# Second half of the scores in a folding bank, and the operand tile 384 bytes further on

## The chip, the cores and the metric

The kernel runs on one core of a Trainium2 chip. The metric is the device time of one execution in microseconds, as the median of several runs. Engines are named as the profile names them: PE is the matrix engine (PEld its weight loads, which overlap its matmuls), DVE the vector engine, ACT the scalar engine, POOL and SP the two others; SP issues all the DMAs here. PSUM is the memory that PE writes, in eight banks of 512 fp32 columns; SBUF is the memory that it reads.

## The reference

Three layers follow one another. Attention goes through 32 memory slots for each of 4 x 8 heads; then come a feed-forward layer with a squared ReLU, and four small feed-forward layers weighted by the probabilities of a domain:

```python
a = softmax(phi, axis=2)                       # (4, 8, 576, 32)
k_m, v_m = a^T k, a^T v                        # (4, 8, 32, 64)
attn = softmax(q k_m^T / 8)                    # (4, 8, 576, 32)
x = heads_joined(attn v_m)                     # (2304, 512)
h = relu(x @ w_in);  x = (h * h) @ w_out       # 512 -> 2048 -> 512
for e in range(4):                             # 512 -> 1024 -> 512 each
    out += p[:, e] * (relu(x @ w1[e]) @ w2[e])
```

## The kernel before

Every large product is made of three matmuls on float32r operands: a value is split into a high part and a rest, and high x high, high x rest and rest x high are summed in PSUM. So each tile of operands holds a high and a low half.

**Stage one** (0 to about 120 us) takes the attention in 8 groups of 4 heads (2 groups for each of the 4 batches). `attention(g)` has a front, up to its `yield`, and a back. The front makes the softmax over phi, transposes it on PE (L132), multiplies it with k and v (L139), transposes that (L156), and makes the scores in two halves of 288 columns (L169, two matmuls each). Each half lands in a bank with the tag `score`, of which there is one, and DVE turns it into the tile `st` (L173). The back is the softmax over the scores on DVE and ACT, up to `at`, which is split into the attention's high part (ACT, L191) and low part (DVE, L192). `fold(s, b)` multiplies v_m into slab s of w_in for batch b: PE matmuls into two banks with the tag `fold` (L296), and a split on ACT and DVE (L302, L303). `first_l1` (L320) multiplies the folded weights with the attention, and `first_l2` (L342) multiplies its squared ReLU with w_out. The string PROGRAM gives the order in which fronts (F), backs (B), folds (A), first-layer pieces (U) and chunks of weights (W) are written; the build's scheduler then puts the instructions of each engine in their final order by the dependences and the free banks. Weights of the first layer come as 64-bit floats that DVE turns into fp32 (L206 to L218), seven instructions a chunk.

**Stage two** (about 120 to 403 us) runs the other slabs of the first layer. **Stage three** (403 us to the end) runs the four domain layers in 16 slabs, each done twice, for 1024 tokens at a time (and 256 left over in the second turn). There `second_pair` makes seven products of 6 matmuls of 512 columns each (L470): the moving operand is one of the slots b11, b21, t1 ... b22, which lie in the tile `mem`, the stationary one is a weight tile `w` or `ws`. `second_rest` (L516) does the same for the tokens left over, 256 columns wide, also from `mem`. `second_l2` (L431) follows, with the weights as moving operand, 512 columns, and DVE adds the outcome to `acc` (L442).

`mem` is the operand tile of all that: 73,728 bytes in each partition of SBUF, first the attention and the folded weights of the 4 batches, later the nine slots of stage three. In the built program of before it begins at byte 17,024 of each partition, which is 33 x 512 + 128; `acc` comes right behind it. All slots are multiples of 8,192 bytes from its beginning, and each of their moving operands is 2,048 bytes long, so each of these starts 128 bytes behind a multiple of 512. The tiles of weights and those of `g`, `gh`, `gl` begin at multiples of 512 (in stage two and three).

Of the kernel before, what the change touches and what calls it, by code (L numbers as in the profile page):

```python
# [12 lines left out]
F32 = mybir.dt.float32  # L13
# [8 lines left out]
NT, DM, DFF, E, F2 = 2304, 512, 2048, 4, 1024  # L22
# [16 lines left out]
def tile_kernel(  # L39
# [11 lines left out]
    const = ctx.enter_context(tc.tile_pool(name="const", bufs=1))  # L51
# [8 lines left out]
    def bank(tag):  # L60
        return ps.tile([128, 512], F32, tag=tag, name=tag, bufs=BANKS[tag])

    ident = const.tile([128, 128], F32, name="ident")
    make_identity(nc, ident)

# [5 lines left out]
    slot = [mem[:, i * 4 * NB:(i + 1) * 4 * NB] for i in range(9)]  # L73
    acc = const.tile([128, NT * KT], F32, name="acc")
    yacc = acc.rearrange("p (k n) -> p k n", k=KT)
    p_sb = const.tile([128, NT // 128, E], F32, name="p_sb")
    p_sum = const.tile([128, NT // 128], F32, name="p_sum")


    FIRST_LOADS = "p0 q0 r0 k0 p1 r1 k1 q1 r2 r3"  # L80
# [1 line left out]


    PROGRAM = (
        "F0 W W F1 B0 A0 B1 F2 U0 W W F3 U1 B2 A1 B3 F4 U2 F5 U3 W B4 A2 B5 F6 U4 W F7 U5 "
        "B6 A3 B7 W U6 W U7"
    )


# [27 lines left out]
    def attention(att, g):  # L117
        b, hg = divmod(g, 2)
        ph, kvt, qt = phs[g], kvs[g], qs[g]
        nmax = att.tile([128, 1], F32, tag="nmax", name="nmax")  # L120
        nc.vector.tensor_reduce(out=nmax, in_=ph, axis=AX.X, op=ALU.max, negate=True)
        esum = att.tile([128, 1], F32, tag="esum", name="esum")
        nc.scalar.activation(ph, ph, AF.Exp, bias=nmax, scale=1.0, accum_out=esum)
        rs = att.tile([128, 1], F32, tag="rs", name="rs")
        nc.vector.tensor_scalar_add(rs, esum, 1e-9)
        nc.vector.reciprocal(rs, rs)
        en = att.tile([128, len(CH), 128], F32, tag="en", name="en", bufs=1)
        pa = bank("turn")
        pb = bank("memory")
        for c, (s0, n) in enumerate(CH):  # L130
            dst = pa[:n, c * 128:(c + 1) * 128] if c < 4 else pb[:n, :128]
            nc.tensor.transpose(dst, ph[:, s0:s0 + n], ident)  # L132
        nc.scalar.copy(en[:, 0:4].rearrange("p c m -> p (c m)"), pa)
        nlast = CH[-1][1]
        nc.scalar.copy(en[:nlast, 4], pb[:nlast, :128])
        kvp = pb[:, 128:256]
        for c, (s0, n) in enumerate(CH):
            for h in range(4):
                nc.tensor.matmul(  # L139
                    kvp[h * M:(h + 1) * M, :2 * D],  # L140
                    en[:n, c, h * M:(h + 1) * M],
                    kvt[c][:n, :, h, :],
                    start=(c == 0),
                    stop=(c == len(CH) - 1),
                )


        kvd = att.tile([128, 2, 2, D], F32, tag="kvd", name="kvd", bufs=1)
        nc.scalar.activation(
            kvd,  # L150
            kvp.rearrange("p (v d) -> p v d", v=2).unsqueeze(2).to_broadcast([128, 2, 2, D]),
            AF.Copy, scale=rs,
        )
        kt = pb[:, 256:512]
        for v in range(2):
            nc.tensor.transpose(kt[:, v * 128:(v + 1) * 128], kvd[:, v].rearrange("p z d -> p (z d)"), ident)  # L156
        bt = bdk[g % 2]
        ktv = kt.rearrange("p (v z e m) -> p v z e m", v=2, z=2, e=2)
        for e in range(2):
            rows = slice(e * D, (e + 1) * D)  # L160
            nc.scalar.copy(bt[rows, :, e * M:(e + 1) * M], ktv[rows, 0, :, e, :])
        rows = slice(hg * D, (hg + 1) * D)
        nc.scalar.copy(vt[rows, b], kt[rows, 128:])
        st = att.tile([128, S // 32, 32], F32, tag="st", name="st", bufs=2)
        stf = st.rearrange("p j m -> p (j m)")
        for z in range(2):
            sc = bank("score")
            for pr in range(2):
                nc.tensor.matmul(  # L169
                    sc[pr * 64:(pr + 1) * 64, :HS], bt[:, pr, :], qt[pr][:, z * HS:(z + 1) * HS],  # L170
                    start=True, stop=True,
                )
            nc.vector.transpose(out=stf[:, z * HS:(z + 1) * HS], in_=sc[:, :HS])  # L173
        yield
        mx = att.tile([128, S // 32], F32, tag="mx", name="mx")
        nc.vector.reduce_max(out=mx, in_=st, axis=AX.X)
        nc.vector.tensor_tensor(
            out=st, in0=st, in1=mx.unsqueeze(2).to_broadcast([128, S // 32, 32]), op=ALU.subtract
        )
        nc.scalar.activation(st, st, AF.Exp, scale=1.0 / math.sqrt(D))  # L180
        sm = att.tile([128, S // 32], F32, tag="sm", name="sm")
        nc.vector.reduce_sum(out=sm, in_=st, axis=AX.X)
        nc.vector.tensor_scalar_add(sm, sm, 1e-9)
        nc.vector.reciprocal(sm, sm)
        nc.vector.tensor_tensor(
            out=st, in0=st, in1=sm.unsqueeze(2).to_broadcast([128, S // 32, 32]), op=ALU.mult
        )
        at = att.tile([128, S], F32, tag="at", name="at", bufs=1)
        nc.vector.transpose(out=at, in_=stf)
        hi = atts[b][:, hg]  # L190
        nc.scalar.copy(hi, at)  # L191
        nc.vector.tensor_tensor(out=atts[b][:, 2 + hg], in0=at, in1=hi.bitcast(F32), op=ALU.subtract)  # L192
# [347 lines left out]
    with tc.tile_pool(name="bdp", bufs=1) as bdp, tc.tile_pool(name="cv", bufs=1) as cv, \  # L540
# [6 lines left out]
        with tc.tile_pool(name="att", bufs=2) as att, tc.tile_pool(name="hp1", bufs=2) as hp, \  # L547
# [3 lines left out]
            def front(g):  # L551
                if g not in phs:
                    phs[g] = load_phi(att, g)
                if g not in kvs:
                    kvs[g] = load_kv(att, g)
                if g not in qs:
                    qs[g] = load_q(g)
                at[g] = attention(att, g)
                next(at[g])
# [129 lines left out]
```

## Time and profile before

| | us |
|---|---|
| median of 3 runs | 1167.53 |
| lowest, highest | 1166.3, 1167.62 |
| time of the profiled execution | 1166.94 |
| its span, first to last instruction | 1164.9 |
| PE busy in it | 1139.3 |
| DVE busy in it | 839.0 |
| ACT busy in it | 494.9 |

The span is the part of the time that the trace shows; 2.0 us of the profiled execution's time lie around it. Busy time is added up over the whole span, so an engine that is busy for 72% of it can still be the one that sets the pace in a stage. An end of a matmul is modelled in the trace, so the pace of matmuls is read from start to start.

### The profile page before, as it was taken

What the parts mean: (1) busy time and instruction counts of PE and PEld (TensorE: products, weight loads), DVE (VectorE), ACT (ScalarE), POOL (GpSimd) and SP (SyncE); (2) the same over time, 40 slices, a digit from 0 to 9 for tenths busy, and PEclk for the clock granted to TensorE, in tenths of its full rate; (3) what the DMA queues carried; (4) which work ended last, traced back from release to release, by engine and by line L of the source; (5) the groups of instructions that cost most, each with busy time, mean ns of one, the idle gap of its engine ahead of it and who ended that gap; (6) DMA issues with size and microseconds to landing.
All of it is one profiled execution on the core that took longest, in us unless ns stands there. A gap on an engine that the chain in (4) does not pass through costs nothing.

```text
span 1164.9 us, 16690 instructions
## 1 busy us (share of the span) xinstructions
PE 1139.3 (98%) x6520; PEld 957.9 (82%) x6520; DVE 839.0 (72%) x1442; ACT 494.9 (42%) x1051; POOL 121.3 (10%) x136
## 2 busy tenths in 40 slices
PE   5899999999999999999999999999999999999998
PEld 2676898999999988888888888888888888888886
DVE  5988999887457667777777778856666666666654
ACT  2666555544466563343433434543333333332321
POOL 0000000001010022121121211211111111121000
PEclk9799999999999999999999999999999999999999
DMA  9751222211000111111111111311111111111002
GB/s 313 237 184 37 73 74 91 74 55 55 1 19 1 54 46 64 37 55 55 55 55 37 55 55 53 110 37 37 37 37 54 37 55 37 37 37 37 19 1 91
DMA packets 25599, 72.68 MB, mean 62 GB/s; under 512 B 2992, under 2 KB 3504, under 8 KB 25520
## 3 DMA queue, kind: packets, MB, share of 16 engines
q1 hardware_dynamic: 25520, 71.61, 18.5%
q8 instruction: 51, 0.84, 0.3%
q14 instruction: 28, 0.23, 0.1%
HBM read 66.88 MB, written 4.72 MB: 61 GB/s over the span
## 4 chain that ended last, share of the span: by engine, by line
PE 91%; DVE 6%; ACT 1%; issue 1%; DMA 1%; SPq 0%; ACTq 0%
PE moe L470 23%; PE fold L431 17%; PE memory L431 8%; PE moe L342 8%; PE turn L431 8%; PE moe L320 4%; PE moe L516 4%; PE score L470 4%; PE turn L342 2%; PE score L342 2%; PE memory L342 2%; PE fold L296 2%; PE memory L320 1%; PE score L320 1%; PE memory L139 1%; DVE acc L350 1%
## 5 line engine op out<-in xcount | busy, mean ns | idle before, releaser
L431 PE MATMUL fold<-w,g 128*128 128x512 f32 x864 | 221.4, 391 | 0.0
L470 PE MATMUL moe<-mem,ws 128*128 128x512 f32 x768 | 201.4, 397 | 0.8 <-DVE c L478 0.8
L431 PEld LDWEIGHTS fold<-w,g 128*128 128x128 f32 x864 | 160.2, 188 | 33.2
L470 PEld LDWEIGHTS moe<-mem,ws 128*128 128x128 f32 x768 | 142.7, 188 | 37.9 <-DVE c L478 5.4
L342 PE MATMUL moe<-gh,wo 128*128 128x288 f32 x576 | 130.8, 298 | 1.2 <-ACT acc L348 0.7
L442 DVE SCALAR_TENSOR_TENSOR acc<-fold,p_sb,acc 128x512 f32<-128x512 f32 x135 | 100.8, 747 | 40.4 <-PE fold L431 40.2
L266 POOL TENSOR_TENSOR s<-ra 128x256 f32<-128x256 f32 x32 | 27.2, 850 | 951.5 <-DVE ws L232 391.3
L483 ACT COPY cc<-moe 128x512 f32<-128x512 f32 x96 | 56.1, 584 | 149.6 <-PE moe L470 149.4
L431 PE MATMUL turn<-w,g 128*128 128x512 f32 x432 | 110.1, 390 | 0.0
L431 PE MATMUL memory<-w,g 128*128 128x512 f32 x432 | 109.9, 390 | 0.0
L452 DVE SCALAR_TENSOR_TENSOR g<-c,g 128x512 fp32r<-128x512 f32 x128 | 97.4, 779 | 16.2 <-ACT g L451 11.8
L451 ACT ACTIVATE g<-c 128x512 fp32r<-128x512 f32 x128 | 80.3, 633 | 67.5 <-DVE c L478 66.8
L478 DVE TENSOR_TENSOR c<-moe,cc 128x512 f32<-128x512 f32 x96 | 66.0, 688 | 57.1 <-ACT cc L483 37.0
L342 PEld LDWEIGHTS moe<-gh,wo 128*128 128x128 f32 x576 | 97.4, 189 | 6.5 <-ACT acc L348 2.5
L431 PEld LDWEIGHTS turn<-w,g 128*128 128x128 f32 x432 | 81.1, 188 | 17.4
L431 PEld LDWEIGHTS memory<-w,g 128*128 128x128 f32 x432 | 81.1, 188 | 17.4
L470 PE MATMUL moe<-mem,w 128*128 128x512 f32 x384 | 95.3, 395 | 0.0
L470 PEld LDWEIGHTS moe<-mem,w 128*128 128x128 f32 x384 | 71.9, 188 | 17.0 <-ACT cc L483 0.2
L342 PE MATMUL moe<-gl,wo 128*128 128x288 f32 x288 | 85.6, 297 | 0.0
L320 PE MATMUL moe<-mem 128*128 128x288 f32 x432 | 75.3, 307 | 7.4 <-ACT mem L191 7.4
L231 ACT CAST w<-rb 128x512 fp32r<-128x512 f32 x64 | 39.9, 623 | 97.5 <-PE memory L431 65.8
L320 PEld LDWEIGHTS moe<-mem 128*128 128x128 f32 x432 | 62.3, 192 | 20.8 <-issue 9.8
(119 smaller groups left out, 1830.3 us busy)
## 6 DMA issues: line engine op xcount, KB each, us to landing
ra<-in_wts SPq DMA_DIRECT2D x32, 512.0 KB, 3.5
rb<-in_wts SPq DMA_DIRECT2D x32, 512.0 KB, 3.5
raw<-in_wts SPq DMA_DIRECT2D x28, 512.0 KB, 3.4
kv<-in_kv SPq DMA_DIRECT2D x28, 256.0 KB, 4.8
acc<-in_qT SPq DMA_DIRECT2D x16, 288.0 KB, 5.2
out<-acc SPq DMA_DIRECT2D x18, 256.0 KB, 2.0
ph<-in_phiT SPq DMA_DIRECT2D x8, 288.0 KB, 4.6
acc<-in_wts SPq DMA_DIRECT2D x4, 512.0 KB, 6.1
```

Of the source, the lines that this page charges most:

```text
L231: nc.scalar.copy(t[:, 0], w)
L266: nc.gpsimd.tensor_tensor(out=t[:, 0], in0=a21, in1=a22, op=ALU.add)
L320: nc.tensor.matmul(ph[:, :HS], folded[b][:, lw + hg, fc], atts[b][:, rx + hg, cs], start=(i == 0), stop=(i == 5))
L342: nc.tensor.matmul(po[:, :HS], w[:, lw], rg[:, f], start=(i == 0), stop=(i == 3 * nf - 1))
L431: nc.tensor.matmul(po, g[f][:, lg, at:at + 128], w[:, rw], start=(i == 0), stop=(i == 3 * NF2 - 1))
L442: nc.vector.scalar_tensor_tensor(out=oa, in0=src, scalar=pe, in1=oa, op0=ALU.mult, op1=ALU.add)
L451: nc.scalar.activation(g[:, 0, :n], c, AF.Relu)
L452: nc.vector.scalar_tensor_tensor(out=g[:, 1, :n], in0=c, scalar=0.0, in1=g[:, 0, :n].bitcast(F32), op0=ALU.max, op1=ALU.subtract)
L470: nc.tensor.matmul(po, wb[lw][k], xb[:, rx, k], start=(first and i == 0), stop=(i == 5), skip_group_check=not first,)
L478: nc.vector.tensor_tensor(out=c, in0=p, in1=q, op=ALU.add)
L483: nc.scalar.copy(c, p)
L516: nc.tensor.matmul(ph[:, :NR], w[f][:, lw, k * 128:(k + 1) * 128], x[:, rx, k], start=(i == 0), stop=(i == 3 * KT - 1),)
```

## The change

Two things change; the third hunk only wraps a string at another word. The second half of a group's scores (z = 1) takes a bank with the tag `fold` in place of the single `score` bank. And the two small tiles `p_sb` and `p_sum` are taken from the pool before `mem` and not behind `acc`. They take 384 bytes (288, and 72 rounded up to 96), so in the built program `mem` begins at byte 17,408, which is 34 x 512, and `acc` moves with it. No other tile moves in SBUF, and the number of instructions with a cost is the same.

```diff
     ident = const.tile([128, 128], F32, name="ident")
     make_identity(nc, ident)
+    p_sb = const.tile([128, NT // 128, E], F32, name="p_sb")
+    p_sum = const.tile([128, NT // 128], F32, name="p_sum")
...
     acc = const.tile([128, NT * KT], F32, name="acc")
     yacc = acc.rearrange("p (k n) -> p k n", k=KT)
-    p_sb = const.tile([128, NT // 128, E], F32, name="p_sb")
-    p_sum = const.tile([128, NT // 128], F32, name="p_sum")
...
         for z in range(2):
-            sc = bank("score")
+            sc = bank("score" if z == 0 else "fold")
```

The scheduler answers with another order of stage one on PE, DVE, ACT and SP; on POOL, and behind stage one on all engines, it stays nearly the same. Three places follow, where a row is a run of equal instructions, a minus stands for before and a plus for the change.

On PE, in the front of group 1 (ph_110 is its phi), the scores of group 0 (bdk_85 is their operand):

```order
 L169 MATMUL score<-acc,bdk_85 64x288 x2
+L169 MATMUL fold<-acc,bdk_85 64x288 x2
 L132 MATMUL turn<-ident,ph_110 128x128 x2
 L132 MATMUL memory<-ident,ph_110 64x128
-L296 MATMUL fold<-wf,vt 32x256
-L169 MATMUL score<-acc,bdk_85 64x288 x2
```

The second half now follows directly on the first, in front of the last transposes of group 1, and the fold of batch 0, which began here, has moved back.

Still on PE, a little further: the scores of group 1 (bdk_86), the fold of batch 0, and the first products of the first layer (moe<-mem) against the front of group 2 (ph_293):

```order
 L169 MATMUL score<-acc,bdk_86 64x288 x2
-L296 MATMUL fold<-wf,vt 32x256 x4
-L169 MATMUL score<-acc,bdk_86 64x288 x2
-L320 MATMUL moe<-mem 128x288 x3
+L169 MATMUL fold<-acc,bdk_86 64x288 x2
+L296 MATMUL fold<-wf,vt 32x256 x8
+L320 MATMUL moe<-mem 128x288 x9
 L132 MATMUL turn<-ident,ph_293 128x128 x4
 L132 MATMUL memory<-ident,ph_293 64x128
-L320 MATMUL moe<-mem 128x288 x3
```

All 8 matmuls of the fold now stand behind both halves of the scores of group 1, and nine first-layer matmuls in place of three stand in front of group 2.

On PE at group 4 (ph_579 is its phi, kv_0_581 the first piece of its k and v); before:

```order
L320 MATMUL moe<-mem 128x288 x2
L342 MATMUL moe<-gh,wo_2_397 128x288
L132 MATMUL turn<-ident,ph_579 128x128 x4
L132 MATMUL memory<-ident,ph_579 64x128
L320 MATMUL moe<-mem 128x288 x3
L139 MATMUL memory<-kv_0_581,en 32x128 x4
```

and of the change, from the transposes of group 4 on (the row with bdk_86 is the first half of the scores of group 3):

```order
L132 MATMUL turn<-ident,ph_579 128x128 x2
L169 MATMUL score<-acc,bdk_86 64x288 x2
L169 MATMUL fold<-acc,bdk_86 64x288 x2
L296 MATMUL fold<-wf,vt 32x256 x4
L132 MATMUL turn<-ident,ph_579 128x128 x2
L132 MATMUL memory<-ident,ph_579 64x128
L296 MATMUL fold<-wf,vt 32x256 x4
L139 MATMUL memory<-kv_0_581,en 32x128 x4
```

The front of group 4 stood behind the first products of batch 1 (the row `L320 ... x2`), and now stands in front of them, around the fold of batch 1.

## Rows read from the trace of the kernel before

**Rows 1.** The page: busy time by engine, and the chain's shares by line.
```profile
PE 1139.3 (98%) x6520; PEld 957.9 (82%) x6520; DVE 839.0 (72%) x1442; ACT 494.9 (42%) x1051; POOL 121.3 (10%) x136
...
PE moe L470 23%; PE fold L431 17%; PE memory L431 8%; PE moe L342 8%; PE turn L431 8%; PE moe L320 4%; PE moe L516 4%; PE score L470 4%; PE turn L342 2%; PE score L342 2%; PE memory L342 2%; PE fold L296 2%; PE memory L320 1%; PE score L320 1%; PE memory L139 1%; DVE acc L350 1%
```

**Rows 2.** Busy time by stretch; columns: stretch, length, busy by engine, PEclk, DMA.
```profile
20.00:40.00 20.00, 14.66 (x130) 9.35 (x123) 17.54 (x39) 10.85 (x29) 0.00 (x0) 0.83 0.71 238
40.00:60.00 20.00, 16.28 (x156) 11.31 (x156) 18.45 (x42) 12.31 (x33) 0.00 (x0) 0.83 0.85 280
60.00:80.00 20.00, 19.85 (x208) 14.91 (x204) 18.50 (x44) 14.88 (x43) 0.00 (x0) 1.00 0.63 196
...
120.00:200.00 80.00, 79.03 (x623) 71.37 (x622) 78.14 (x176) 44.01 (x116) 0.00 (x0) 1.00 0.24 79
...
403.00:722.00 319.00, 319.00 (x1391) 260.19 (x1390) 240.86 (x338) 129.64 (x221) 66.03 (x64) 1.00 0.16 52
722.00:1165.00 443.00, 438.17 (x2073) 362.32 (x2071) 284.67 (x428) 145.09 (x252) 47.15 (x56) 1.00 0.13 45
```

**Rows 3.** All waits of PE from 403 to 1160 us: total, times, longest.
```profile
PE moe L470 <- DVE c L478: 0.8, 1, 0.8
```

**Rows 4.** Timeline of PE around 430 us: start, length, instruction, count.
```profile
427.23 1.54 PE L431 MATMUL fold<-w,g 128*128 128x512 f32 x6
...
432.68 1.55 PE L470 MATMUL moe<-mem,ws 128*128 128x512 f32 x6
...
441.07 1.54 PE L431 MATMUL fold<-w,g 128*128 128x512 f32 x6
```

**Rows 5.** Timeline of PE around 1110 us.
```profile
1103.70 1.60 PE L516 MATMUL moe<-mem,w 128*128 128x256 f32 x12
1105.14 1.55 PE L431 MATMUL fold<-w,g 128*128 128x512 f32 x6
...
1110.62 2.96 PE L470 MATMUL moe<-mem,w 128*128 128x512 f32 x12
...
1117.61 1.54 PE L431 MATMUL fold<-w,g 128*128 128x512 f32 x6
```

**Rows 6.** The chain that ended last, around 222 us: start, length, piece, count.
```profile
221.71 1.60 PE moe L342 x12
223.30 1.60 PE score L342 x12
```

**Rows 7.** Busy time by stretch of L470 alone (PE, then PEld).
```profile
403.00:722.00 319.00, 160.22 (x666) 124.71 (x666) 1.00 0.16 52
722.00:1165.00 443.00, 167.81 (x678) 125.94 (x678) 1.00 0.13 45
```

**Rows 8.** Timeline from 14 to 35 us; in brackets idle time before, and what ended it.
```profile
14.55 1.23 PE L169 MATMUL score<-acc,bdk 128*64 128x288 f32 x4
...
17.52 1.23 PE L169 MATMUL score<-acc,bdk 128*64 128x288 f32 x4
...
18.80 0.48 DVE L173 STREAM_TRANSPOSE st<-score 128x288 f32<-128x288 f32 x1 [1.44 <-PE score L169]
...
29.81 1.09 PE L320 MATMUL moe<-mem 128*128 128x288 f32 x3 [4.54 <-ACT mem L191]
...
34.86 1.06 PE L320 MATMUL moe<-mem 128*128 128x288 f32 x6
```

**Rows 9.** Timeline from 52 to 55 us.
```profile
52.13 0.85 PE L320 MATMUL moe<-mem 128*128 128x288 f32 x2 [2.89 <-ACT mem L191]
...
53.02 1.06 PE L132 MATMUL turn<-ident,ph 128*128 128x128 f32 x4
...
54.94 2.52 PE L139 MATMUL memory<-kv,en 128*32 128x128 f32 x40
```

**Rows 10.** The chain that ended last, around 95 us.
```profile
93.80 0.69 PE fold L296 x14
...
96.48 0.40 PE score L320
```

More of the change, by code (lines that the diff above doesn't have):

```diff
@@ L75, in tile_kernel @@
     yacc = acc.rearrange("p (k n) -> p k n", k=KT)
-    p_sb = const.tile([128, NT // 128, E], F32, name="p_sb")
-    p_sum = const.tile([128, NT // 128], F32, name="p_sum")
     FIRST_LOADS = "p0 q0 r0 k0 p1 r1 k1 q1 r2 r3"
     PROGRAM = (
-        "F0 W W F1 B0 A0 B1 F2 U0 W W F3 U1 B2 A1 B3 F4 U2 F5 U3 W B4 A2 B5 F6 U4 W F7 U5 "
-        "B6 A3 B7 W U6 W U7"
+        "F0 W W F1 B0 A0 B1 F2 U0 W W F3 U1 B2 A1 B3 F4 U2 F5 U3 W B4 A2 B5 F6 U4 W F7 U5 B6 "
+        "A3 B7 W U6 W U7"
     )
```

## The prediction

> **What bounds the kernel now.** I read the page first. PE is busy 1139.3 of 1164.9 us, DVE 839.0, and the longest shares of the chain are matmul lines: L470 with 23 and 4%, L431 with 17, 8 and 8% [rows 1]. Then busy time by stretch, since a share over the span mixes stages [rows 2]. In stage three (403 us to the end) PE is busy 319.00 of 319 and 438.17 of 443 us, DVE 76% and 64%. All that PE waited for there is one wait of 0.8 us [rows 3]. So PE sets the pace of two thirds of the time, and a nanosecond on a matmul of that stage is a nanosecond on the end. In stage one it is otherwise: from 20 to 80 us PE is idle 5.34, 3.72 and 0.15 us, and DVE only 2.46, 1.55 and 1.50 us [rows 2]. DVE is close to full there, PE waits for what DVE makes, and the granted clock of PE falls to a mean of 0.83 in two of the stretches. From 120 to 200 us both are full (79.03 and 78.14 of 80), so time won in stage one stays won only as far as DVE is ahead as well.
>
> The last view is the pace of the matmuls, from start to start. In stage three L431 and L470 have the same shape, 512 columns on 128 rows. Around 430 us, 24 of L431 take 427.23 to 432.68, which is 227.1 ns each; the 36 of L470 behind them take 432.68 to 441.07, 233.1 ns each [rows 4]. Around 1110 us it is 24 in 5.48 us (228.3) and 30 in 6.99 us (233.0) [rows 5]. At the full clock of 2.4 GHz, which the rows grant here (1.00), 512 columns are 213.3 ns. So L431 has 13.8 ns on top, and L470 19.8. The narrower lines have what L431 has: 12 of L342 take 1.59 us, 132.5 ns for 288 columns, 12.5 on top [rows 6]; 12 of L516 take 1.44 us, 120.0 ns for 256 columns, 13.3 on top [rows 5]. L470 alone is out of line, by about 6 ns.
>
> **The tile moved by 384 bytes.** L470 reads its moving operand from `mem`, 2,048 bytes that begin 128 bytes behind a multiple of 512, so that they touch five blocks of 512 bytes. The moving operand of L431 is a weight tile at a multiple of 512 and touches four. The change makes L470's four as well. L470 and L431 differ in other things too, the banks among them, but L342 writes `moe` and `score` as L470 does [rows 6], and has no excess. The rate of L470 is also the same at 433 and at 1110 us, beside other work on ACT and DVE. That leaves the place of the operand as the likeliest cause, and it is bounded by the rows so:
> - No gain, if the place doesn't matter. L516 reads the same slots' tile from the same offset (its rows of 256 columns touch three blocks where two would do) and has no excess, and L342 with 288 columns has none either.
> - The whole excess. There are 666 + 678 = 1344 matmuls of L470 [rows 7]. At L431's pace near them they gain 6.0 ns in the first part (666 x 6.0 = 4.0 us) and 4.7 ns in the second (678 x 4.7 = 3.2 us), 7.2 us together; at 227.1 ns throughout, 1344 x 6.0 = 8.1 us.
>
> I take -7.6 us. The form that is nearest to L470 after the change is L431 (same columns, same offset), not L516, whose operand is half as long: none of the lines without an excess touches more than four blocks. Nothing hides PE in that stage [rows 3], and DVE at 76% of the first part would be at 77% of one that is 4 us shorter, so it does not become the bound.
>
> A rule of the Trainium skill speaks against this term. "SBUF — State Buffer", section "Specifications (TRN2)", gives lines of 16 bytes as what a read can cross; byte 17,024 and byte 17,408 both begin such a line, so by it nothing would change. The trace is at odds with it as far as L470 and L431 differ; no row here shows one tile at two offsets.
>
> Other users of `mem` and `acc` move with it: L320 reads offsets of 0, 128, 256 and 384 alike from both kernels (its pieces are 1,152 bytes), so it keeps its mix. I price it at nothing, and the vector work on `acc` too, since DVE has a quarter free where `acc` is used.
>
> **The bank of the second half.** The first half of group 0 runs 14.55 to 15.78; the second starts at 17.52, behind transposes and two folds, and is turned by DVE at 18.80 [rows 8]. In the change the second follows at once, ends near 15.78 + 1.23 = 17.01, and DVE can turn it at about 17.05, 1.75 us sooner. With the softmax behind it on DVE and ACT, the first product of the first layer, which waited until 29.81 (PE idle 4.54 us), may start some 2 us sooner. But group 2's transposes come from a softmax of phi that stands in DVE's queue no earlier than before, so what PE gains is that six of its matmuls that ran at 34.86 are done ahead: 6 x 133 ns, 0.8 us. At group 4, the front stood behind the wait that ended at 52.13 (2.89 us idle) and now stands ahead of it: five transposes and 40 small matmuls, which took 1.06 and 2.52 us from 53.02 on, at the low clock [rows 9]. They can fill that wait if phi and kv of group 4 have landed, so 0 to 2.9 us. DVE's work is the same in sum and it was idle 1.55 us from 40 to 60 and 5.5 us from 20 to 80 [rows 2]; stage one can gain no more than that 5.5.
>
> Against it, the fold now waits for the second half to be turned, since both use the two folding banks, and PE's queue behind the fold waits with it (the front of the next group, the first layer's matmuls). For batch 0 there is cover: its fold ended near 25 us, and its user at 29.81 was waiting for something else. At the last fold there is none: from 93.80 to 96.48 the fold, its split on ACT and DVE and the next product are on the chain [rows 10], 2.7 us, which could be paid twice. So stage one is between -5.5 and +2.7 us; I take -1.0, nearest to the 0.8 us that I can follow, for the DVE queue is full.
>
> **Sum.** 1166.94 - 7.6 - 1.0 = 1158.3 for a profiled execution. The median of the runs shown is 0.6 above that execution, so 1158.9.
>
> **The rivals.**
> - *The place doesn't matter* (the rule above as a mechanism: L470's excess comes from something else about it, its weights or the way it steps through the slots). For it: L516 and L342. Against it: nothing else that L470 shares with no other line is in the rows. Then only stage one is left: 1167.5 - 1.0 = 1166.5, not to be told from before.
> - *Slower: the fold behind the scores.* Each group's fold or score must find a folding bank free, for which a pair of scores (0.71 us at the full clock, 1.23 at the low one [rows 8]) and a turn of 0.48 us go by. In eight groups without cover that is 8 x 1.19 = 9.5 us, in half of them 4.8. For it: the chain at 95 us. Against it: two of the waits that I followed have over 2 us of cover. It decides the sign from 2.3 us on if the place doesn't matter, and from 9.9 us on if it does. With half of the groups and no gain in L470: 1172.3.
> - *Faster still: stage one loses its two stalls.* If both waits (4.54 and 2.89 us) close as far as DVE allows, 5.5 us and not 1.0: 1154.4. For it: PE's order at group 4, and the clock, which was at 0.83 behind these waits. Against it: DVE's 17.54, 18.45 and 18.50 of 20 us.
>
> **How the numbers follow.** The forecast gets 0.66, the place that doesn't matter 0.20, the slower case 0.06, the faster one 0.08. About 0.2% (2.3 us) is what a measurement of this kernel can tell from no change, as the runs lie within 1.3 us. The forecast's own range is 1158.9 with 4 us to either side (half of stage one's bounds, and 0.4 us of the first term). The range over the cases reaches down to 1153.5, below the case with both stalls gone, and up to 1167.5, which holds most of the second case and leaves its upper third and the slower case out, some 0.14. Faster: nearly all of 0.66 (0.64), 0.08, and a third of the second case (0.06), 0.78 together. Same: 0.12 of the second case and 0.02, 0.14. Slower: 0.06 and 0.02 of the second.
>
> **What would show it.** L470 at 227 to 229 ns from start to start, so that 36 of them around 430 us take 8.2 and not 8.39 us, and L516 and L342 at their old 120 and 133 ns: then the first term is right. L470 still at 233: the place is not the cause. The length from the first L470 to the end shorter by 7 to 8 us: it reaches the end. For stage one, the second L169 of group 0 in a folding bank near 15.8 and its turn near 17.05; the first L320 near 27.8; no wait of 2.9 us near 50 us; and a first L470 about 1 us sooner than now (403 us). If the waits of PE for L296 grow, or the first L470 starts later than now, the folding banks have cost more than I think. The prediction is wrong if L470 keeps its pace, or if stage one loses more than some 5 us.

## The result, and the profile after

| | before | after |
|---|---|---|
| median (4 runs each) | 1167.16 us | 1154.83 us |
| lowest, highest | 1166.3, 1167.62 | 1154.55, 1156.35 |
| profiled execution, its span | 1166.94, 1164.9 | 1155.03, 1153.2 |

The ratio is 0.9896, with a 95% interval of 0.9884 to 0.9908: 12.3 us faster. The forecast was 1158.9 with a range of 1153.5 to 1167.5, so the time lies in the range, 4.1 us below the forecast. The changed kernel was timed again later, beside other kernels: 1156.61, ratio 0.9903 [0.9888, 0.9917], 11.0 us.

The page of the changed kernel, PE's busy time and the chain's shares (compare [rows 1]):

```profile
PE 1128.9 (98%) x6520; PEld 957.8 (83%) x6520; DVE 836.9 (73%) x1442; ACT 492.8 (43%) x1051; POOL 120.9 (10%) x136
PE moe L470 23%; PE fold L431 17%; PE moe L342 9%; PE memory L431 8%; PE turn L431 8%; PE moe L320 5%; PE moe L516 4%; PE score L470 4%; PE turn L342 3%; PE score L342 2%; PE memory L342 2%; PE fold L296 2%; PE memory L320 1%; PE score L320
```

The same 6520 matmuls keep PE busy for 10.4 us less, and the span is 11.7 us shorter. PE is still the bound; nearly all of the gain is matmuls that take less time, not waits that went away. Busy time by stretch (length, then PE, PEld, DVE, ACT, POOL, granted clock, DMA share and GB/s), against [rows 2]:

```profile
20.00:40.00 20.00, 15.64 (x97) 8.91 (x98) 14.88 (x34) 8.01 (x21) 0.00 (x0) 0.52 0.65 225
40.00:60.00 20.00, 19.30 (x191) 13.85 (x189) 17.74 (x42) 14.91 (x42) 0.00 (x0) 0.96 0.72 234
60.00:80.00 20.00, 17.77 (x194) 13.52 (x191) 19.52 (x44) 14.20 (x41) 0.00 (x0) 1.00 0.72 243
...
403.00:722.00 319.00, 319.00 (x1413) 263.98 (x1413) 243.31 (x346) 131.81 (x222) 65.56 (x64) 1.00 0.16 53
722.00:1165.00 443.00, 426.36 (x2035) 355.99 (x2033) 277.41 (x416) 140.31 (x244) 47.22 (x56) 1.00 0.12 43
```

In the 319 us from 403 on, PE is as full as before and runs 1413 matmuls where 1391 were. Its pace, from the timeline of PE around 430 and 1095 us (start, length, instruction, count), against [rows 4, 5]:

```profile
424.06 1.52 PE L431 MATMUL fold<-w,g 128*128 128x512 f32 x6
...
429.50 1.52 PE L470 MATMUL moe<-mem,ws 128*128 128x512 f32 x6
...
437.66 1.52 PE L431 MATMUL fold<-w,g 128*128 128x512 f32 x6
...
1092.64 1.59 PE L516 MATMUL moe<-mem,w 128*128 128x256 f32 x12
1094.07 1.55 PE L431 MATMUL fold<-w,g 128*128 128x512 f32 x6
...
1099.54 2.88 PE L470 MATMUL moe<-mem,w 128*128 128x512 f32 x12
...
1104.98 1.30 PE L470 MATMUL moe<-mem,ws 128*128 128x512 f32 x5
```

The 36 of L470 now take 429.50 to 437.66, 8.16 us or 226.7 ns each (8.39 and 233.1 before). Late in the stage 24 of them take 5.44 us, 226.7 each (233.0 before). L431 stays: 24 in 5.44 us (226.7), and 24 in 5.47 us (227.9, behind L516). L516 stays at 1.43 us for 12, 119.2 ns. Over all start-to-start times in the two traces (those over 400 ns left out, which are waits), the mean of L470 falls from 234.14 to 228.46 ns, and that of L431 from 228.03 to 227.19.

The chain around 220 us shows L342 as it was in [rows 6], 132.5 ns:

```profile
218.71 1.59 PE moe L342 x12
220.30 1.60 PE score L342 x12
```

And all waits of PE from 400 to 1150 us (in total, times, longest), against [rows 3]:

```profile
PE moe L470 <- DVE c L478: 1.0, 1, 1.0
```

Stage one, from the timeline (idle time before in brackets), against [rows 8 to 10]:

```profile
14.64 1.23 PE L169 MATMUL score<-acc,bdk 128*64 128x288 f32 x4
...
15.65 1.17 PE L169 MATMUL fold<-acc,bdk 128*64 128x288 f32 x4
...
16.92 0.47 DVE L173 STREAM_TRANSPOSE st<-fold 128x288 f32<-128x288 f32 x1
...
21.46 1.23 PE L169 MATMUL score<-acc,bdk 128*64 128x288 f32 x4 [0.62 <-issue]
...
26.99 2.74 PE L320 MATMUL moe<-mem 128*128 128x288 f32 x9 [1.60 <-ACT mem L191]
...
49.46 0.84 PE L139 MATMUL memory<-kv,en 128*32 128x128 f32 x18
...
54.11 0.53 PE L320 MATMUL moe<-mem 128*128 128x288 f32 x2 [0.36 <-ACT mem L191]
...
92.63 0.62 PE L296 MATMUL fold<-wf,vt 64*32 64x256 f32 x2 [1.45 <-DVE mem L303]
```

The second half of group 0 starts at 15.65 and not at 17.52, its turn at 16.92 and not at 18.80. The first L320 starts at 26.99 behind an idle time of 1.60, where 4.54 stood. Of the wait of 2.89 us near 52 us, 0.36 is left at 54.11: matmuls of group 4's front (L139) and of the first layer run there. In exchange the wait of a fold for `mem` near 92 us is 1.45 us long, where before one of 0.96 and one of 0.49 stand between 95 and 97 us:

```profile
95.36 0.64 PE L296 MATMUL fold<-wf,vt 64*32 64x256 f32 x8 [0.96 <-DVE mem L303]
96.48 0.40 PE L320 MATMUL score<-mem 128*128 128x288 f32 x1 [0.49 <-ACT mem L302]
```

Put together, the two profiled executions differ so: up to the first L470, 403.55 against 400.73 (2.8 us); from there to the end, 1164.9 - 403.55 = 761.35 against 1153.2 - 400.73 = 752.47 (8.9 us). That sum is the span's 11.7.

### The profile page after: what moved, and what is told of

Its sections match the earlier page's. It is cut to its first block, busy times and chain, and to the rows that moved or that the text cites. A ratio compares the mean times of both kernels' runs of the same rounds, so it can differ in the third digit from the quotient of the medians.

```text
span 1153.2 us, 16692 instructions
## 1 busy us (share of the span) xinstructions
PE 1128.9 (98%) x6520; PEld 957.8 (83%) x6520; DVE 836.9 (73%) x1442; ACT 492.8 (43%) x1051; POOL 120.9 (10%) x136
## 4 chain that ended last, share of the span: by engine, by line
PE 92%; DVE 4%; ACT 1%; issue 1%; DMA 0%; SPq 0%; ACTq 0%
PE moe L470 23%; PE fold L431 17%; PE moe L342 9%; PE memory L431 8%; PE turn L431 8%; PE moe L320 5%; PE moe L516 4%; PE score L470 4%; PE turn L342 3%; PE score L342 2%; PE memory L342 2%; PE fold L296 2%; PE memory L320 1%; PE score L320 1%; PE turn L320 1%
## 5 line engine op out<-in xcount | busy, mean ns | idle before, releaser
L431 PE MATMUL fold<-w,g 128*128 128x512 f32 x864 | 220.6, 390 | 0.0
L470 PE MATMUL moe<-mem,ws 128*128 128x512 f32 x768 | 197.3, 392 | 1.0 <-DVE c L478 1.0
L431 PEld LDWEIGHTS fold<-w,g 128*128 128x128 f32 x864 | 160.2, 188 | 31.9
L470 PEld LDWEIGHTS moe<-mem,ws 128*128 128x128 f32 x768 | 142.8, 188 | 35.0 <-DVE c L478 5.8
L342 PE MATMUL moe<-gh,wo 128*128 128x288 f32 x576 | 131.4, 298 | 0.3 <-ACT acc L348 0.3
L431 PE MATMUL turn<-w,g 128*128 128x512 f32 x432 | 109.8, 389 | 0.0
L431 PE MATMUL memory<-w,g 128*128 128x512 f32 x432 | 109.6, 389 | 0.0
L452 DVE SCALAR_TENSOR_TENSOR g<-c,g 128x512 fp32r<-128x512 f32 x128 | 96.0, 769 | 16.2 <-ACT g L451 11.7
L342 PEld LDWEIGHTS moe<-gh,wo 128*128 128x128 f32 x576 | 97.1, 188 | 4.9 <-ACT acc L348 1.9
L431 PEld LDWEIGHTS memory<-w,g 128*128 128x128 f32 x432 | 81.1, 188 | 16.9
L431 PEld LDWEIGHTS turn<-w,g 128*128 128x128 f32 x432 | 81.1, 188 | 16.9
L470 PE MATMUL moe<-mem,w 128*128 128x512 f32 x384 | 93.0, 389 | 0.0
L342 PE MATMUL moe<-gl,wo 128*128 128x288 f32 x288 | 85.2, 296 | 0.0
L470 PEld LDWEIGHTS moe<-mem,w 128*128 128x128 f32 x384 | 71.9, 188 | 15.0 <-ACT cc L483 0.2
L320 PE MATMUL moe<-mem 128*128 128x288 f32 x432 | 75.4, 308 | 3.9 <-ACT mem L191 3.2
L329 DVE TENSOR_TENSOR gl<-g,gh 128x288 fp32r<-128x288 f32 x128 | 59.4, 467 | 26.0 <-ACT gh L328 25.1
```

Source lines behind the costliest of these rows:

```text
L320: nc.tensor.matmul(ph[:, :HS], folded[b][:, lw + hg, fc], atts[b][:, rx + hg, cs], start=(i == 0), stop=(i == 5))
L329: nc.vector.tensor_tensor(out=gl[:, f], in0=g, in1=gh[:, f].bitcast(F32), op=ALU.subtract)
L342: nc.tensor.matmul(po[:, :HS], w[:, lw], rg[:, f], start=(i == 0), stop=(i == 3 * nf - 1))
L431: nc.tensor.matmul(po, g[f][:, lg, at:at + 128], w[:, rw], start=(i == 0), stop=(i == 3 * NF2 - 1))
L452: nc.vector.scalar_tensor_tensor(out=g[:, 1, :n], in0=c, scalar=0.0, in1=g[:, 0, :n].bitcast(F32), op0=ALU.max, op1=ALU.subtract)
L470: nc.tensor.matmul(po, wb[lw][k], xb[:, rx, k], start=(first and i == 0), stop=(i == 5), skip_group_check=not first,)
```

## The experiments

The first two rows are the result above. Each of the other times stands beside runs of the kernel before on the same chip, whose medians were all 1167.6 us. The last two columns are of the profiled execution: the start of the first L470, and the length from there to the end of the span. That length turned out to be the sharpest measure: it lies within 0.4 us for all kernels that treat the operands of stage three alike, whatever happens in stage one.

| kernel | median, us | ratio [95%] | first L470 | from there to the end |
|---|---|---|---|---|
| before | 1167.16 | 1 | 403.55 | 761.35 |
| the change | 1154.83 | 0.9896 [0.9884, 0.9908] | 400.73 | 752.47 |
| the change, again | 1156.61 | 0.9903 [0.9888, 0.9917] | 403.08 | 752.42 |
| the tile alone | 1158.96 | 0.9923 [0.9910, 0.9935] | 402.91 | 752.69 |
| the bank alone | 1165.23 | 0.9978 [0.9968, 0.9987] | 402.54 | 761.26 |
| weights at 128 | 1164.32 | 0.9972 [0.9962, 0.9982] | 400.57 | 761.23 |
| tile at 256 | 1156.67 | 0.9905 [0.9891, 0.9919] | 402.94 | 752.56 |
| all at 128 | 1157.40 | 0.9901 [0.9885, 0.9918] | 403.44 | 752.46 |
| hidden values 32 apart | 1165.59 (one run) | | 401.70 | 761.80 |
| hidden values 96 apart | 1164.71 (one run) | | 402.40 | 760.20 |
| fold bank first | 1155.80 | 0.9892 [0.9876, 0.9908] | 402.41 | 752.79 |
| `moe` as second bank | 1158.39 | 0.9926 [0.9908, 0.9944] | 402.68 | 752.82 |
| fold bank in group 0 only | 1157.53 | 0.9905 [0.9887, 0.9923] | 403.14 | 752.56 |
| fold bank in groups 1 to 7 | 1155.94 | 0.9896 [0.9883, 0.9909] | 402.01 | 752.49 |

An offset below is the byte at which an operand begins in its partition, modulo 512. In a matmul of L431 and L470 two operands come from SBUF: the stationary one, 128 columns that PEld loads (512 bytes in a partition), and the moving one, 512 columns (2,048 bytes). For L470 the moving one is `mem` and the stationary one a weight tile; for L431 it is a weight tile that moves, and the hidden values `g` (L450) are stationary.

### The tile alone

```diff
     # against the changed kernel
-            sc = bank("score" if z == 0 else "fold")
+            sc = bank("score")
```

> The tile at a multiple of 512 bytes alone; the scores keep the one bank, and the order of instructions is that of the kernel before. Theory (place of the operand): L470 goes from 233 to 227 ns from start to start, 1344 of them give 8 to 9 us, the first L470 still starts near 403.6 us as in the kernel before; about 1158.3 us, 0.992 of before. Rival (the gain of L470 comes with the new order or the banks): L470 stays at 233 ns, 1167 us.

Measured: 0.9923, 8.65 us. The two stalls of before are still there, and L470 has the new pace:

```profile
17.59 1.23 PE L169 MATMUL score<-acc,bdk 128*64 128x288 f32 x4
...
29.32 1.09 PE L320 MATMUL moe<-mem 128*128 128x288 f32 x3 [4.54 <-ACT mem L191]
...
51.37 0.85 PE L320 MATMUL moe<-mem 128*128 128x288 f32 x2 [2.89 <-ACT mem L191]
...
431.67 1.52 PE L470 MATMUL moe<-mem,ws 128*128 128x512 f32 x6
...
439.83 1.52 PE L431 MATMUL fold<-w,g 128*128 128x512 f32 x6
```

36 of L470 in 8.16 us, with the instructions in the order of before. So the place of the tile gives the pace, and the pace gives 8.7 us (761.35 to 752.69).

### The bank alone

```diff
     # against the kernel before
-            sc = bank("score")
+            sc = bank("score" if z == 0 else "fold")
```

> The bank of the second half alone; the tile stays 128 bytes behind a multiple of 512, and the order is that of the changed kernel. Theory: L470 at 233 ns as before, the first L470 near 400.7 us as in the changed kernel, so 2.8 us less than before and no more: 1164.3 us, 0.9976. Rival (the bank carries the whole gain): L470 at 227 ns, 1155 us.

Measured: 0.9978, 2.4 us. L470 at the old pace, 8.39 us for 36:

```profile
431.65 1.55 PE L470 MATMUL moe<-mem,ws 128*128 128x512 f32 x6
...
440.04 1.31 PE L431 MATMUL fold<-w,g 128*128 128x512 f32 x5
```

The two parts add up: 8.65 + 2.4 = 11.0, beside 12.3 and 11.0 for both at once.

### Weights at 128

This asks whether the offset of the moving operand alone counts, as the prediction has it. Everything behind `acc` (weights and `g`) goes 128 bytes on; `mem` stays where the change put it.

```diff
-    acc = const.tile([128, NT * KT], F32, name="acc")
+    acc = const.tile([128, NT * KT + 32], F32, name="acc")[:, :NT * KT]
```

> The changed kernel with all tiles behind acc moved by 128 bytes (weights, g, gh, gl), mem stays at a multiple of 512. Theory (a moving operand of 512 columns off a multiple of 512 bytes is slow, whichever line): L431, whose moving operand is a weight tile, goes from 227 to 233 ns, 1728 of them cost 10 us; L470 stays at 227, since only its stationary operand has moved; about 1165 us. Rival (it is the offset between stationary and moving operand): L431 stays at 227, as both of its operands move alike, and L470 goes to 233 ns, which costs 8.5 us; about 1163.5 us.

```profile
425.63 1.52 PE L431 MATMUL turn<-w,g 128*128 128x512 f32 x6
...
429.71 1.55 PE L470 MATMUL moe<-mem,ws 128*128 128x512 f32 x6
...
438.10 1.54 PE L431 MATMUL fold<-w,g 128*128 128x512 f32 x6
```

L470 is back at 8.39 us for 36, with its moving operand still at a multiple of 512. L431, whose moving weight tile now begins at 128 and so touches five blocks of 512, keeps its pace: 18 in 4.08 us, 226.7 ns each. Both are the opposite of what the prediction's cause says. What the slow cases share is that the two operands of one matmul have different offsets.

### Tile at 256, and all at 128

The first puts `mem` and `acc` at 256 and leaves weights and `g` at 0. The second puts all of them at 128, so that no operand is at a multiple of 512, but the two of a matmul agree.

```diff
 # tile at 256
-    p_sum = const.tile([128, NT // 128], F32, name="p_sum")
+    p_sum = const.tile([128, 88], F32, name="p_sum")[:, :NT // 128]
-    acc = const.tile([128, NT * KT], F32, name="acc")
+    acc = const.tile([128, NT * KT + 64], F32, name="acc")[:, :NT * KT]
 # all at 128
-    p_sum = const.tile([128, NT // 128], F32, name="p_sum")
+    p_sum = const.tile([128, 56], F32, name="p_sum")[:, :NT // 128]
```

> The changed kernel with mem and acc 256 bytes behind a multiple of 512, all other tiles at multiples of 512. Theory (512 columns that touch five blocks of 512 bytes in place of four): L470 at 233 ns again, 8.5 us slower than the changed kernel, 1163.4 us. Rival (a grid of 256 bytes is enough): L470 at 227 ns, 1154.9 us.

> The changed kernel with mem, acc and every tile behind them 128 bytes on, so that stationary and moving operands of L470 and of L431 lie at equal offsets again, but none at a multiple of 512. Theory (what counts is whether the stationary and the moving operand agree in the place within 256 bytes): L470 and L431 at 227 ns, as in the changed kernel, 1155 to 1156.5 us. Rival (the moving operand must be at a multiple of 512, or of 256): both at 233 ns, 8 + 10 us more, 1173 us.

The tile at 256:

```profile
431.73 1.52 PE L470 MATMUL moe<-mem,ws 128*128 128x512 f32 x6
...
439.89 1.30 PE L431 MATMUL fold<-w,g 128*128 128x512 f32 x5
```

All at 128:

```profile
432.22 1.52 PE L470 MATMUL moe<-mem,ws 128*128 128x512 f32 x6
...
440.38 0.84 PE L431 MATMUL fold<-w,g 128*128 128x512 f32 x3
```

8.16 us for 36 in both. No multiple of 512 is needed for either operand, and offsets that differ by 256 are as good as equal ones.

### Hidden values 32 and 96 bytes apart

`mem` and the weights stay as in the change, and the six buffers of `g` get 32 (or 96) bytes of padding each. So L431's stationary operand stands at 0, 32, 64, 96, 128, 160 (or 0, 96, 192, 288, 384, 480), and its moving operand at 0. Two theories were open: only the half of 256 bytes matters in which an operand begins, or any difference does.

```diff
-        g = hp3[0].tile([128, 2, NB], F32R, tag="g", name="g")
+        g = hp3[0].tile([128, 2 * NB + 8], F32R, tag="g", name="g")[:, :2 * NB].rearrange(
+            "p (h n) -> p h n", h=2)                     # + 24 for 96 bytes
```

> The changed kernel with the six buffers of g, the stationary operand of L431, 32 bytes further apart: they lie at 0, 32, 64, 96, 128 and 160 bytes behind a multiple of 512, the moving operand at 0. Theory (the two operands differ in which 128-byte half of 256 bytes they start): L431 at 227 ns for the first four offsets, at 233 to 234 for 128 and 160; a third of the 1728 is slow, 3.5 us more than the changed kernel. Rival (any difference costs): 227 ns for offset 0 alone, 8.6 us more. Rival (the place of the moving operand alone): 227 ns for all.

> The same with buffers 96 bytes further apart: offsets 0, 96, 192, 288, 384 and 480. Theory of the 128-byte halves: 227 ns at 0, 96 and 288, 233 to 234 at 192, 384 and 480; half of the 1728 slow, 5 us more than the changed kernel. Rival (any difference modulo 512 costs): only offset 0 at 227 ns, 8.6 us more.

Around 430 us with 96 bytes, where 24 of L431 take 425.91 to 431.50, 5.59 us or 232.9 ns each, and L470 behind them 8.16 us for 36:

```profile
425.91 1.56 PE L431 MATMUL fold<-w,g 128*128 128x512 f32 x6
...
431.50 1.52 PE L470 MATMUL moe<-mem,ws 128*128 128x512 f32 x6
...
439.66 1.53 PE L431 MATMUL fold<-w,g 128*128 128x512 f32 x6
```

The slow line has changed places: now L431 pays and L470 doesn't. Mean start-to-start times of L431 by the offset of `g`, in ns, where the next matmul reads the same buffer of `g` (1148 of the 1728, by the buffers of the built program): with 96 bytes 0: 227.4; 96: 233.0; 192: 231.1; 288: 232.0; 384: 232.3; 480: 234.1. With 32 bytes 32: 232.5; 64: 233.8; 96: 231.7; 128: 232.3; 160: 234.5, and 230.4 at 0, which is slower than with 96 bytes although both operands agree. So the buffers beside it seem to matter too; how, no run here shows. Every difference tried that is no multiple of 256 costs 4 to 7 ns against the 227.2 of the changed kernel, so the theory of the halves fell. With 96 bytes the mean rises by 231.63 - 227.19 = 4.4 ns, which is 7.7 us over 1728 matmuls; the stage is 760.20 - 752.47 = 7.7 us longer.

### Where the folding bank's gain comes from

Five kernels with the tile as in the change. The first is the change itself, once more; the others alter which bank the halves take.

```diff
-            sc = bank("score" if z == 0 else "fold")
+            sc = bank("fold" if z == 0 else "score")              # fold bank first
+            sc = bank("score" if z == 0 else "moe")               # moe as second bank
+            sc = bank("fold" if z and g == 0 else "score")        # group 0 only
+            sc = bank("fold" if z and g else "score")             # groups 1 to 7
```

> The changed kernel once more, as the measure for the two runs beside it: 1155 us, 0.9896 of before, or a little more, as the two parts alone sum to 0.9923 - 0.0022 = 0.990.

> The changed kernel with the two banks swapped: the first half of the scores goes to a folding bank, the second to the score bank. Nothing waits for the one bank either, but the scheduler makes another order of it. Theory (the second half no longer waits for the first, and that is the gain of 2.5 to 4 us in stage one): as the changed kernel within 1 us. Rival (the gain is what this one order happened to give): off by more than 2 us to either side.

> The changed kernel with the second half of the scores in one of the three banks tagged moe, so that the folds keep their two banks to themselves and the first layer shares its three. Theory (no wait for the one bank is what counts): as the changed kernel within 1 us. Rival (the order that the scheduler made counts, or the folds' and first layer's wait for banks): off by more than 2 us; near tile_only's 1159 us if the gain is lost.

> The changed kernel with the folding bank for the second half of group 0 alone; the other seven groups keep both halves in the score bank. The operand tile stays where the change put it, so the part on the tile is worth 0.9923 here, and the whole change 0.990. Theory (the early stall at group 0 carries the gain of the bank): 0.990 or below, first L320 near 27 us, a wait near 50 us comes back but costs nothing at the first L470. Rival (the later groups carry it): 0.992, first L470 as with the tile alone (402.9 us or later).

> The changed kernel with the folding bank for the second half of groups 1 to 7, and group 0 with both halves in the score bank. Theory (the stall at group 0 carries the gain of the bank): 0.992, as the tile alone, with the second L169 of group 0 near 17.5 us again. Rival (the later groups carry it): 0.990. Third possibility, both parts are within what two programs of this kind differ by anyway: both kernels between 0.990 and 0.9925 with overlapping intervals, and the bank's gain can't be divided.

Which half takes the folding bank makes no difference (0.9892 beside 0.9896 and 0.9903). With `moe` as the second bank, no half waits for the other and no fold for a half (though the first layer's products use `moe` too), yet the ratio is 0.9926, as with the tile alone; its runs scatter from 1156.18 to 1162.42 us. The median is 1.8 us above that of the change timed beside it, which neither of the two expected outcomes foresaw. There the scheduler has put the next group's transposes ahead of the first layer's products, and PE waits for the softmax of phi, twice:

```profile
28.28 1.12 PE L132 MATMUL turn<-ident,ph 128*128 128x128 f32 x4 [5.17 <-ACT ph L123]
...
53.20 0.66 PE L132 MATMUL turn<-ident,ph 128*128 128x128 f32 x4 [2.68 <-ACT ph L123]
```

With the folding bank in group 0 only, the first L320 starts at 27.24, and a wait of 1.63 us remains where the second stall was:

```profile
27.24 0.66 PE L320 MATMUL moe<-mem 128*128 128x288 f32 x3 [3.28 <-ACT mem L191]
...
54.92 0.71 PE L320 MATMUL moe<-mem 128*128 128x288 f32 x2 [1.63 <-ACT mem L191]
```

With it in groups 1 to 7, the first L320 starts hardly later, although group 0 uses one bank. The scheduler has put the second half of group 0 at 16.67, and not near 17.5 as was expected:

```profile
16.67 1.23 PE L169 MATMUL score<-acc,bdk 128*64 128x288 f32 x4
...
27.47 1.09 PE L320 MATMUL moe<-mem 128*128 128x288 f32 x3 [2.84 <-ACT mem L191]
```

The ratios (0.9905 and 0.9896) lie on either side of the change's 0.9903, with intervals that overlap each other and the change's. That of the tile alone, 0.9910 to 0.9935, overlaps with group 0 only, and just misses groups 1 to 7 (up to 0.9909). This is nearly the third of the expected outcomes: the runs lean to groups 1 to 7, but six executions of the one and four of the other don't divide the bank's 2.4 us. The wait that is tied to a part is the second: it is 1.63 us with the folding bank in group 0 only.

None of the kernels beats the changed one by more than the intervals allow.

## Why the prediction was right, and where it was not

**The first term: right in sign, near in size, wrong in its cause.** Forecast were 7.6 us, from 1344 matmuls that lose their excess over L431. The mean of L470 fell by 5.68 ns, and 1344 x 5.68 = 7.6 us. The length from the first L470 to the end fell by 8.7 us with the tile alone and 8.9 with the whole change, not by 7 to 8. The sum left out that L431 gains as well, where it stands beside an L470: 0.84 ns in the mean, 1728 x 0.84 = 1.5 us. The first six L431 behind an L470 fall from 229.4 to 226.7 ns, while those from the 13th on keep 226.7. Together that is 9.1, near the 8.9 seen.

The step that failed is the one that named "the place of the operand" as the cause: five blocks of 512 bytes touched by the moving operand, where L431's touch four. Weights at 128 gave L470 four blocks and the old pace, and L431 five blocks and the good pace; all at 128 gave both five and both the good pace. What the runs show in its place is a relation between the moving operand and the stationary ones. Where their offsets agree modulo 256 bytes, matmuls of 512 columns follow each other at 226.7 ns in a long run, else at 231 to 235 in the mean. (The first two L431 behind an L516 take 233 to 236 ns even in the changed kernel, where all offsets agree.) Before the change L470 had 128 against 0. The forecast came out by luck: moving `mem` to a multiple of 512 also made it agree with the weights. That it is their relation, and not either place, is shown by weights at 128, all at 128 and the two kernels with padded hidden values. What in the chip makes the pair slow was not found. Nor do the runs tell whether the moving operand has to agree with its own stationary operand or with that of the next matmul, which PEld can load meanwhile. In all but the padded kernels the two have one offset; there, some 230 matmuls in each agree with one of them only, and both kinds are slow (231 ns where only the next agrees, 233 where only the own does).

**What spoke against the term.** The prediction let L516 and L342, which have no excess, speak for a case without gain. L516 keeps 119 to 120 ns and L342 133 in the kernels above, although L516 reads `mem` at 128 against weights at 0 before the change, and more than half of L342's pieces of `gh` and `gl` start 64, 128 or 192 bytes off its weights modulo 256 (in the built program of the change). So the mean pace of 256 and 288 columns does not show a difference of offsets, and these rows were no evidence on 512 columns. (Single steps of L516 do show it: from the seventh on behind an L431 they scatter from 117 to 122 ns before the change, and all read 120 after it.) The rule of the Trainium skill that was weighed there ("SBUF — State Buffer", section "Specifications (TRN2)": what a read can cross is a line of 16 bytes) does not account for what was measured: all offsets tried are multiples of 32, and the pace still differs by 4 to 7 ns.

**Other users of `mem` and `acc`** were priced at nothing. The tile alone has both stalls of stage one as long as before (4.54 and 2.89 us) and L342 and L320 at 133 ns; nothing of a price is seen.

**The bank: right in its steps, too small in size.** The forecast had the second L169 at 15.8, its turn at 17.05, the first L320 at 27.8, and no wait near 50 us; measured are 15.65, 16.92, 26.99 and 0.36 us. The 26.99 is one of a spread: in the eight traces with this order of instructions the first L320 starts between 25.76 and 28.92, in the two with one bank at 29.32 and 29.81. The term was -1.0, and the bank alone is worth 2.4 us (1.5 to 3.7 by its interval); that is the step that was mis-sized. The profiled executions alone leave it less sharp: the first L470 starts at 400.57 to 403.44 in eight executions with both halves' banks as in the change (mean 402.2), and at 402.91 and 403.55 in two with one bank. The same program differed by 2.35 us between two executions (400.73 and 403.08). Of that, 0.59 us is there at the first scores (14.64 and 15.23) and another 1.3 at those of group 1 (21.46 and 23.39), between which 40 L139 take 1.43 us in the one and 2.52 in the other. All executions together are sharper. Each span less the length that the same kernel's trace has from the first L470 to the end is an estimate of where the first L470 started: 404.4 us in the mean of 53 executions with one bank (the kernel before and the tile alone), and 401.7 in 35 with the folding bank (the change, the change again, the bank alone, weights at 128, tile at 256, all at 128), 2.7 us apart. So of the 12.3 us of the first timing about 1 is the luck of the executions, 8.7 the tile, and 2 to 3 the bank.

**The slower rival**, the fold behind the scores, is seen in one place: 1.45 us near 92 us, instead of 0.96 and 0.49. It adds nothing to PE's idle time there. **The faster rival**, both stalls closing as far as DVE allows, saw the stalls rightly and not what follows: they did close, to 1.6 and 0.4 us, but other waits opened, and PE's idle time from 20 to 80 us fell only from 9.21 to 7.29 us (4.36, 0.70 and 2.23 in the three stretches). DVE's busy time fell as well, from 17.54 to 14.88 us between 20 and 40 us, so it was not DVE that had become full there.

## What to carry to other kernels

Compare start-to-start times of matmuls of one shape across lines; where one line is some nanoseconds behind, look at the places of both its operands, not of one. In these kernels, 512-column matmuls on float32r operands with a weight load each keep their best pace when stationary and moving operand begin at the same offset modulo 256 bytes, which padding of a small tile ahead of them can arrange. And take a change of several parts apart before its cause is believed: here a right number rested on a wrong reason, and one run with the weights moved instead of the tile told them apart.

## What the hardware showed that was not expected

Besides the offsets: the granted clock that the profile shows and the pace of the matmuls don't always agree. Busy time around 20 us in the changed kernel (columns as above):

```profile
17.00:20.00 3.00, 2.09 (x43) 1.17 (x42) 3.00 (x6) 0.86 (x3) 0.00 (x0) 1.00 1.02 415
21.00:24.00 3.00, 2.54 (x12) 1.05 (x16) 1.83 (x5) 0.52 (x3) 0.00 (x0) 0.50 1.02 370
24.00:30.00 6.00, 4.13 (x25) 2.43 (x17) 5.68 (x11) 2.85 (x6) 0.00 (x0) 0.50 0.54 185
```

The same from 24 to 30 us with the bank alone, which has the same order of instructions there:

```profile
24.00:30.00 6.00, 4.40 (x28) 1.95 (x25) 5.21 (x11) 1.43 (x4) 0.00 (x0) 1.00 0.62 209
...
28.41 2.74 PE L320 MATMUL moe<-mem 128*128 128x288 f32 x9 [1.60 <-ACT mem L191]
```

And of the kernel before, the stretch from 17 to 20 us and the scores of group 1:

```profile
17.00:20.00 3.00, 3.00 (x34) 1.52 (x36) 1.56 (x4) 0.22 (x2) 0.00 (x0) 1.00 1.04 408
...
23.21 0.71 PE L169 MATMUL score<-acc,bdk 128*64 128x288 f32 x4
```

The granted clock reads 0.50 in the changed kernel and 1.00 with the bank alone, but the nine L320 take 2.74 us in both. From start to start five of their eight steps are 240 ns in both, which is 288 columns at 1.2 GHz; from 120 us on a step is 133 ns. The pace is what to read. By the pace, the changed kernel runs group 1's scores at the low level, 1.23 us for four at 21.46, where the kernel before took 0.71 us at 23.21. From 17 to 20 us PE had been busy 2.09 us in the changed kernel, and 3.00 in the kernel before. That alone does not settle it: with weights at 128, where the order of instructions is the same, it was busy 2.15 us, and the same four took 0.71 us at 21.63. The six other traces with this order have 1.23. So some of what the second bank wins in waits is given back in slower matmuls; how much, no run here separates.
